# Moving the first chunk's gate into the second chunk, and reordering the loads of w_mod, q and the third chunk, in a long-convolution and token-mixer kernel

## The chip, the cores and the metric

The kernel runs on one core of a Trainium2 chip. The core has a matrix engine (TensorE, PE in the profile, with its weight loads as PEld), a vector engine (VectorE, DVE), a scalar engine (ScalarE, ACT), a general engine (GpSimd, POOL) and a queue engine that issues transfers (SyncE, SP). Each works through its own list of instructions in order; they wait for one another by semaphores. The metric is the device time of one execution in microseconds. Before the change the median of three runs was 666.49 us (665.19 to 666.98). One further execution was taken with the hardware profiler: 671.21 us, of which 669.4 us are the span that the trace covers.

## The reference

Everything is float32, one batch, 2048 tokens, 640 channels. What is computed, cut to what matters:

```python
mod = (silu(c) @ w_mod).reshape(1, 6, 1, 640)            # six rows: sa, ca, ga, sb, cb, gb
h = layernorm(q) * (1 + ca) + sa
k_shift = sum(k shifted by t, times shift_k[:, t])        # four taps along the tokens
kv = k_shift * v
y = irfft(rfft(kv, 4096) * rfft(ssm_k, 4096))[:2048] + kv * ssm_D
x = q + ga * (h * y)
h = layernorm(x) * (1 + cb) + sb
x = x + gb * token_mlp(h)                                 # 2048 -> 1728 -> 2048 along the tokens, gelu between
```

The change touches only the first half, up to `x = q + ga * (h * y)`.

## The kernel before, in words

The 640 channels are five **chunks** of 128. The long convolution of a chunk is a transform of length 64 by 32, done with small matrix products on TensorE. A chunk goes through these stages; all of them are small Python functions that append instructions to the engines' lists, so the order in which they are called is the order on each engine (no scheduler changes it).

- `kv_ops` (VectorE, and one group in four on GpSimd) multiplies the taps, sums, and multiplies by v: eight instructions for each of four groups; the result lies in the tile `x` (X in the code).
- `step1(0, t)`, t = 0 to 3 (line 230): first forward step on kv. `step1(1, t)`: the same on the filter, which `perm` (line 177, ScalarE) has permuted from the tile `aux` (KSR) into `p` after `perm_add` (GpSimd) has put ssm_D into its first element. ScalarE evacuates each step to `z` (line 235).
- `f2(g)`, g = 0 to 7 (line 249): the second forward step, called the products below. For each group ScalarE copies one half to `kt` (line 255), VectorE makes two products into `p` (two buffers of it in turn), GpSimd adds them to `y`. So VectorE's product of group g waits for GpSimd's addition of group g - 2. Between the products VectorE works off a list `fill`, a share of it in each group: in the first, second and third chunk this is `kv_ops` for the next chunk.
- `i2(0)`, `i2(1)` (line 280): the inverse by 32 in two halves, evacuated by ScalarE (line 288). `i1(0)`, `i1(1)` (line 300): the inverse by 64.
- `gate`: VectorE multiplies that result by a tile A1, which holds layernorm(q) for the chunk, scaled and shifted by two rows G1 and G0; then q gets it added, and `spill` writes the chunk's columns out.

A1 comes from 16 ScalarE copies (line 307) with the statistics of q as scale and bias, and two passes of VectorE over it with G1 and G0. G0 and G1 come from w_mod: `mod_part` (line 364) multiplies five row blocks of w_mod by silu(c), `mod_sum` (line 368) copies the sum out, `mod_row` (lines 375 to 384) spreads a row over the partitions. The statistics of q (bn_stats, line 600) are 48 VectorE instructions, and `rstd` turns them into scale and bias (a square root on ScalarE, then five small VectorE instructions).

TensorE's results lie in three PSUM tiles used in rotation (`psum()`), so a stage waits until the tile three stages back is read. A1 is one half of the tile `aux`, the filter (KSR) the other; w_mod's third and fourth blocks were loaded over both.

SyncE issues nearly all loads, strictly in order. In the first chunk it issues q (32 transfers), w_mod (five), the second inverse matrix `v1`, the second chunk's filter, then k and v of the third chunk. All forward and inverse stages of chunk c and the forward steps of chunk c + 1 are called in the loop body of chunk c.

Of the kernel before, what the change touches and what calls it, by code (L numbers as in the profile page):

```python
# [11 lines left out]
AF = mybir.ActivationFunctionType  # L12
ALU = mybir.AluOpType

S, D, F = 2048, 640, 1728
DC = 128
# [34 lines left out]
def mixer_kernel(ctx: ExitStack, tc: tile.TileContext, q, k, v, shift_k, ssm_k, ssm_D, w1, b1, w2, b2, c,  # L51
# [462 lines left out]
    all_taps()  # L514
    load_taps(2)
# [10 lines left out]
    three = lambda t: [t[:, 640 * j:640 * j + 640] for j in range(3)]  # L526
    pl = [three(t) for t in (T_v1, T_v1[:, 1920:3840], T_aux, T_aux[:, 2048:3968], P)]

    def load_q():
        for j in range(16):  # L530
            for b in range(2):
                sync.dma_start(XH[j // 8][64 * b:64 * b + 64, j % 8], dram(q, (16 * b + j) * D, [[32 * D, 64], [1, D]]))  # L532
        for kk in range(4):
            mod_load(0, kk, (T_v1[:, 0:1920], T_v1[:, 1920:3840], T_aux[:, 0:1920], T_aux[:, 2048:3968])[kk])
# [8 lines left out]
    for c in range(NC):  # L543
# [3 lines left out]
        for g in range(8):  # L547
# [21 lines left out]
            if c == 0 and g < 4:  # L569
                lay_w2(1, g)  # L570
                if g == 3:
                    load_q()
# [24 lines left out]
        if c == 0:  # L597
            for j in range(16):
                for h in range(2):
                    dve.bn_stats(bst[:, j, h, :], XR(j, 320 * h, 320))  # L600
                dve.bn_aggr(mv[:, j, :], bst[:, j, 0:2, :])
# [4 lines left out]
        if c == 0:  # L606
            mod_load(0, 4, P[:, 0:1920])
            for t in range(4):
                step1(0, t)
            ps = psum()  # L610
            pe.transpose(ps[:, 0:36], stg, ID[0:36, 0:36])
            act.activation(cols, ps[:, 0:36], AF.Copy)
            act.activation(sil, cols[:, 30:35], AF.Silu)
            i2(0)
            for kk in range(4):
                mod_part(tap, kk, pl[kk])
                if kk == 1:
                    sync.dma_start(T_v1[:, 0:4096], c_v1, max_dma_last_dim=4096)
                if kk == 2:
                    load_ks(1)  # L620
            rstd(rs1, nm1, 0, 16)
            run(ac[0:4])
            i2(1)
            mod_part(tap, 4, pl[4])
# [9 lines left out]
            mod_sum(tap, T_kt[:, 0:640])  # L634
            run(ac[4:8])
# [3 lines left out]
            for i in range(3):  # L639
                mod_row(i, T_kt[:, 0:640])  # L640
            run(ac[8:16])
            run(po)
            perm(1)
            taps()
            load_taps(3)
            load_ks(2)
            fill.extend(kv(3, ((0,), (1, 2), (3,))))
        elif cn is not None:
            for t in range(2):
                step1(0, t)  # L650
# [58 lines left out]
        if c == 0:  # L709
            add_x(c, 0)  # L710
            add_x(c, 1)
        spill(c)
        if c:
            k0()
        for t in range(1 if c else 0, 4):
            step1(1, t)
        if cn == NC - 1:
            dv(12)
            fill.extend(x1s(c, j) for j in range(16))
        else:  # L720
            dv(11 if c else 8)
# [505 lines left out]
```

## Time and profile before

| what | value |
|---|---|
| median of three runs | 666.49 us (665.19 to 666.98) |
| profiled execution | 671.21 us, span 669.4 us |
| TensorE matmul busy in the span | 619.5 us (93%) |
| VectorE busy | 501.9 us (75%) |
| ScalarE busy | 309.7 us (46%) |
| GpSimd busy | 108.1 us (16%) |
| mean granted TensorE clock | 0.982 of full |

These shares are means over the whole program. In the page's strip of 40 slices TensorE is below nine tenths only within the first thirteen; the five chunks run there, and the token MLP after them keeps it busy to the end. A row of the timeline gives the start in us, the length in us, the engine, the line, the operation, the tiles written and read, the shapes and how many instructions were merged; in brackets the idle time before it and what ended it. A row of the chain of waits gives start, length and what the chain ran through.

### The profile page before, as it was taken

Reading aid. Unit: us, or ns where it says so; the run is one execution under the profiler, and the core shown is the slowest. Engines: PE = TensorE matmul, PEld = TensorE weight load, DVE = VectorE, ACT = ScalarE, POOL = GpSimd, SP = SyncE. Lnnn points to the kernel's source line nnn. Section 1 sums busy time; section 2 is a strip of 40 time slices with the busy share of each in tenths; the row PEclk is TensorE's granted clock in tenths of the full one; section 3 lists DMA queues with packets and bytes.
Section 4 is the critical chain, followed back from the end, with each engine's and each line's share of the span. In section 5 each row is a group of like instructions: output and inputs, shape, how many; then the busy total and the mean of one; then the engine's idle time right before and its main releaser. Section 6 shows DMA issues by size and latency. Waiting matters only on the chain.

```text
span 669.4 us, 20749 instructions
## 1 busy us (share of the span) xinstructions
PE 619.5 (93%) x9073; PEld 597.8 (89%) x9073; DVE 501.9 (75%) x860; ACT 309.7 (46%) x483; POOL 108.1 (16%) x120
## 2 busy tenths in 40 slices
PE   0599878899998999999999999999999999999997
PEld 0598568788997989689999999999999999999997
DVE  6688569969969948789974213846689889888886
ACT  0574475545735647667765224334243332333331
POOL 5284027413324127000000000000000000000000
PEclk9999789999999999879999999999999999999999
DMA  9968988727438525414006630885598565345601
GB/s 179 213 194 225 391 172 159 168 54 165 83 70 221 180 51 156 172 33 95 0 1 126 119 71 1 189 234 144 174 365 268 173 179 154 102 144 169 188 31 41
DMA packets 175472, 98.01 MB, mean 146 GB/s; under 512 B 89843, under 2 KB 165398, under 8 KB 175126
## 3 DMA queue, kind: packets, MB, share of 16 engines
q1 hardware_dynamic: 170834, 95.38, 54.0%
q10 hardware_dynamic: 4548, 1.31, 1.1%
q8 instruction: 71, 1.16, 0.7%
q14 instruction: 19, 0.16, 0.1%
HBM read 79.63 MB, written 19.14 MB: 148 GB/s over the span
## 4 chain that ended last, share of the span: by engine, by line
PE 71%; DVE 16%; DMA 6%; issue 3%; SPq 2%; ACT 1%; POOL 0%; ACTq 0%; DVEq 0%; POOLq 0%
PE pst L1128 26%; PE pst L463 19%; PE pst L230 9%; PE pst L249 7%; PE pst L280 5%; PE pst L993 4%; DVE tap L60 3%; DVE kt L60 2%; DMA aux<-in_A_ssm_k_dram 2%; PE pst L300 2%; DMA aux<-in_w_mod_dram 2%; DVE p L60 1%; SPq L532 1%; PE tap L364 1%; DMA in<-in_A_k_dram 1%
## 5 line engine op out<-in xcount | busy, mean ns | idle before, releaser
L249 PE MATMUL pst<-z,w 128*64 128x64 f32 x2560 | 78.9, 223 | 11.0 <-DVE p L60 6.0
L249 PEld LDWEIGHTS pst<-z,w 128*64 128x64 f32 x2560 | 76.8, 138 | 13.7 <-issue 10.4
L230 PE MATMUL pst<-v,x 128*64 128x128 f32 x640 | 45.7, 302 | 24.2 <-DVE x L60 23.7
L230 PEld LDWEIGHTS pst<-v,x 128*64 128x64 f32 x640 | 43.6, 221 | 24.9 <-POOL t L488 23.7
L235 ACT ACTIVATE z<-pst 128x1024 f32<-128x1024 f32 (+2 forms) x45 | 41.4, 931 | 43.6 <-PE pst L230 24.9
L60 POOL TENSOR_TENSOR y<-p 128x256 f32<-128x256 f32 x72 | 54.1, 776 | 40.1 <-DVE p L60 39.7
L60 DVE TENSOR_TENSOR p<-pst,kt 128x512 f32<-128x512 f32 x80 | 50.8, 681 | 10.5 <-ACT kt L255 9.6
L280 PEld LDWEIGHTS pst<-v,y 32*128 32x128 f32 x1280 | 39.4, 193 | 4.2 <-issue 2.7
L280 PE MATMUL pst<-v,y 32*128 32x64 f32 x1280 | 41.2, 279 | 1.6 <-issue 1.0
L255 ACT ACTIVATE kt<-pst 128x512 f32<-128x512 f32 x40 | 23.9, 598 | 36.7 <-PE pst L249 20.9
L230 PE MATMUL pst<-v,p 128*64 128x128 f32 x640 | 37.3, 274 | 1.4 <-ACT p L177 1.2
L230 PEld LDWEIGHTS pst<-v,p 128*64 128x64 f32 x640 | 35.3, 137 | 2.2 <-ACT p L177 1.4
L1128 PE MATMUL pst<-r_z,m_w 128*128 128x320 f32 x198 | 37.2, 309 | 0.0
L60 DVE TENSOR_TENSOR tap<-tap,kt 128x512 f32<-128x512 f32 x51 | 35.5, 696 | 1.3
L60 DVE TENSOR_TENSOR kt<-in,tap 128x512 f32<-128x512 f32 x51 | 34.9, 685 | 1.5
L300 PEld LDWEIGHTS pst<-z,v 64*64 64x64 f32 x1280 | 24.7, 157 | 7.9 <-issue 3.5
L1128 PEld LDWEIGHTS pst<-r_z,m_w 128*128 128x128 f32 x198 | 31.1, 188 | 0.0
L300 PE MATMUL pst<-z,v 64*64 64x64 f32 x1280 | 26.9, 243 | 3.7 <-issue 2.4
L288 ACT ACTIVATE z<-pst 128x512 f32<-128x512 f32 x38 | 21.3, 664 | 18.3 <-PE pst L280 18.3
L1065 ACT ACTIVATE m_w<-m_v 128x896 fp32r<-128x896 f32 x19 | 17.9, 948 | 23.3 <-DVE m_v L60 13.0
L60 DVE TENSOR_TENSOR m_w<-m_v,m_w 128x896 fp32r<-128x896 f32 x19 | 20.6, 1086 | 6.5 <-ACT m_w L1065 6.5
L1128 PE MATMUL pst<-h_x,m_w 128*128 128x320 f32 x132 | 24.6, 309 | 0.0
(303 smaller groups left out, 1417.2 us busy)
## 6 DMA issues: line engine op xcount, KB each, us to landing
x<-in_B_w_dram SPq DMA_DIRECT2D x18, 512.0 KB
m_v<-in_B_w_dram SPq DMA_DIRECT2D x20, 384.0 KB
aux<-in_A_ssm_k_dram SPq DMA_DIRECT2D x10, 512.0 KB
out_dram<-m_w SPq DMA_DIRECT2D x32, 160.0 KB
in<-in_A_k_dram SPq DMA_DIRECT2D x36, 128.0 KB
in<-in_A_v_dram SPq DMA_DIRECT2D x36, 128.0 KB
ts<-m_p SPq DMA_DIRECT2D x10, 320.0 KB
m_w<-xs SPq DMA_DIRECT2D x20, 160.0 KB
```

The costliest lines, as they stand in the source:

```text
L60: TT = lambda eng, o, a, b, op: eng.tensor_tensor(o, a, b, op=op)
L230: pe.matmul(ps.rearrange("p (b m a) -> p b a m", b=2, a=4)[64 * ri:64 * ri + 64, a // 4, a % 4], lhs, F1[:, 128 * ri:128 * ri + 128], star ...
L235: act.activation(Z[:, side, t, :, k0:k1], ps.rearrange("p (b k a) -> p b k a", b=4, a=4)[:, :, k0:k1], AF.Copy)
L249: pe.matmul(pk[64 * h:64 * h + 64, kk // 4, ri, kk % 4], W2[k1 // 32][:, 2 * (k1 % 32) + ri], rhs, start=True, stop=True)
L255: act.activation(halves_(kt), pv[:, :, 1], AF.Copy)
L280: pe.matmul(pp[qd // 2][:, o:o + 64], Y[p, ri, i:i + 2].rearrange("p i k -> p (i k)"), V2[p, 64 * ri:64 * ri + 64], start=ri == 0, stop=ri ...
L288: act.activation(o, i, AF.Copy)
L300: pe.matmul(ps[64 * b:64 * b + 64, 512 * e + 64 * jj:512 * e + 64 * jj + 64], V1[p, ri, n2], T2[p, :, 32 * ri + n2], start=ri == 0, stop=r ...
L463: pe.matmul(ps[0:m, h, 0:320], w_.bitcast(F32R), r_[:, 320 * h:320 * h + 320].bitcast(F32R), start=first and i == 0, stop=last and i == 2)
L993: pe.matmul(ps[n][:, h, 0:320], sets[n][:, j].bitcast(F32R), r[:, 320 * h:320 * h + 320].bitcast(F32R), start=j == 0 and r is hh, stop=j = ...
L1065: act.activation(W[n][0].bitcast(F32R), A[p, w_], AF.Copy)
L1128: pe.matmul(bank[n], w[:, i].bitcast(F32R), r.bitcast(F32R), start=m == 0 and k == 0, stop=m == 6 and k == 2)
```

## The change

- The five w_mod blocks are loaded before q, into the place of `v1`, into half of q's own place (`xa`) and into A1's place; the second chunk's filter is loaded right after them. q comes after the third chunk's k and v, its second half of rows first (QJ), and after it k and v of the fourth chunk and the third chunk's filter.
- The sum over w_mod now stands in one piece in front of the first chunk's inverse, in a PSUM tile of the rotation.
- The first chunk's inverse by 64 is not gated. ScalarE copies it to A1's place (line 734). The statistics of q are taken in the second chunk: nine rows of tokens ahead of its products, seven as `fill`. `kv_ops` for the third chunk moves from `fill` to the time before the second chunk's products.
- After the second chunk's products, `rstd` runs, and ScalarE makes 16 copies for the first chunk (`late_rows`, line 549) into the free tiles `t` and `kt`; VectorE gates with them (`late_gate`, six instructions), GpSimd adds to q, `spill(0)` follows. Then come the second chunk's own 16 copies into A1, which before stood two by two between its products.

```diff
     all_taps()
+    PL = (T_v1[:, 0:1920], T_v1[:, 1920:3840], T_x[0][:, 0:1920], T_x[0][:, 1920:3840], T_aux[:, 2048:3968])
+    pl = [three(t) for t in PL]
+    for kk in range(5):
+        mod_load(0, kk, PL[kk])
+    load_ks(1)
     load_taps(2)
...
+    QJ = (*range(8, 16), *range(8))
     def load_q():
-        for j in range(16):
+        for j in QJ:
...
+    def late_rows(half):
+        for i in range(8):
+            j = 8 * half + i
+            act.activation(G_[half][:, i], XR(j, 0, DC), AF.Identity, scale=rs1[:, j:j + 1], bias=nm1[:, j:j + 1])
+    def late_gate(half):
+        a = G_[half]
+        g = lambda G: G[:, None, 0:DC].to_broadcast([128, 8, DC])
+        TT(dve, a, a, g(G1), ALU.mult)
+        TT(dve, a, a, g(G0), ALU.add)
+        av = a.rearrange("p j (m e) -> p e j m", e=2)
+        y = T_aux[:, 2048 + 1024 * half:3072 + 1024 * half]
+        TT(dve, av, y.rearrange("p (e j m) -> p e j m", e=2, j=8), av, ALU.mult)
+        x = XH[half][:, :, 0:DC]
+        TT(pool, x, x, a, ALU.add)
...
-            if c:
+            if c > 1:
                 n_ = 2 if cn is not None else 3
                 for f_ in ac[n_ * g:n_ * g + n_]:
                     f_()
...
             taps()
             load_taps(3)
+            ps = psum()
+            pe.transpose(ps[:, 0:36], stg, ID[0:36, 0:36])
+            act.activation(cols, ps[:, 0:36], AF.Copy)
+            act.activation(sil, cols[:, 30:35], AF.Silu)
+            for t in range(4):
+                step1(0, t)
+            ps = psum()
+            for kk in range(5):
+                mod_part(ps, kk, pl[kk])
+                if kk == 1:
+                    sync.dma_start(T_v1[:, 0:4096], c_v1, max_dma_last_dim=4096)
+            load_q()
+            mod_sum(ps, T_kt[:, 0:640])
+            perm(1)
+            i2(0)
+            for i in range(2):
+                mod_row(i, T_kt[:, 0:640])
+            ops = kv(3, ((0,), (1, 2), (3,)))
+            run(ops[0:16])
+            mod_row(2, T_kt[:, 0:640])
+            i2(1)
+            run(ops[16:])
             load_ks(2)
-            fill.extend(kv(3, ((0,), (1, 2), (3,))))
+            for j in QJ[0:9]:
+                run(q_stats(j))
+            for j in QJ[9:]:
+                fill.extend(q_stats(j))
         elif cn is not None:
-            for t in range(2):
-                step1(0, t)
+            if c == 1:
+                rstd(rs1, nm1, 0, 16)
+            step1(0, 0)
+            if c == 1:
+                late_rows(0)
+            step1(0, 1)
+            if c == 1:
+                late_rows(1)
+                for half in range(2):
+                    late_gate(half)
+                spill(0)
+                run(ac)
             perm(cn)
...
             ps = i1(half)
+            if c == 0:
+                act.activation(T_aux[:, 2048 + 1024 * half:3072 + 1024 * half], ps, AF.Copy)
+                continue
```

**Where the instructions stand now.** On SyncE, after the small loads of the first chunk (line 511 loads c), the queue before went on like this; lines 532 and 537 load q, 357 w_mod, 618 and 650 the matrix v1, 165 and 167 ssm_D and the filter, 161 the taps, 145, 151 and 156 k and v:

```order
L511 DMA g<-in_c_dram 5x128
L161 DMA rows<-in_A_shift_k_dram 64x256 x2
L532 DMA xa<-in_A_q_dram 64x640 x16
L532 DMA xb<-in_A_q_dram 64x640 x16
L357 DMA v<-in_w_mod_dram 128x3x640 x2
L357 DMA aux<-in_w_mod_dram 128x3x640 x2
L357 DMA p<-in_w_mod_dram 128x3x640
L618 DMA v<-in_const_v_dram 128x4x1024
L165 DMA rows<-in_A_ssm_D_dram 1x64 x2
L167 DMA aux<-in_A_ssm_k_dram 64x64x32 x2
```

The same place in the changed kernel:

```order
L511 DMA g<-in_c_dram 5x128
L357 DMA v<-in_w_mod_dram 128x3x640 x2
L357 DMA xa<-in_w_mod_dram 128x3x640 x2
L357 DMA aux<-in_w_mod_dram 128x3x640
L165 DMA rows<-in_A_ssm_D_dram 1x64 x2
L167 DMA aux<-in_A_ssm_k_dram 64x64x32 x2
L161 DMA rows<-in_A_shift_k_dram 64x256 x2
L145 DMA in<-in_A_k_dram 64x8x64 x4
L151 DMA in<-in_A_v_dram 64x8x64 x2
```

w_mod and the second chunk's filter have moved past all of q, and the taps of the third chunk (161) now stand behind the filter.

Further on in the same queue of the changed kernel, from the second half of q to the third chunk's filter:

```order
L537 DMA xa<-in_A_q_dram 64x640 x16
L151 DMA in<-in_A_v_dram 64x8x64 x2
L156 DMA in<-in_A_k_dram 63x3x64 x2
L145 DMA in<-in_A_k_dram 64x8x64 x2
L151 DMA in<-in_A_v_dram 64x8x64 x2
L145 DMA in<-in_A_k_dram 64x8x64 x2
L151 DMA in<-in_A_v_dram 64x8x64 x2
L145 DMA in<-in_A_k_dram 64x8x64 x2
L151 DMA in<-in_A_v_dram 64x8x64 x2
L145 DMA in<-in_A_k_dram 64x8x64 x2
L165 DMA rows<-in_A_ssm_D_dram 1x64 x2
L167 DMA aux<-in_A_ssm_k_dram 64x64x32 x2
```

Ahead of this filter load (167) now stand 32 transfers of q and 18 of the fourth chunk's k and v; before, it followed directly on the taps of line 161 and had the 18 behind it.

On ScalarE, from the last copy of the second chunk's products (line 255) to the evacuation of its second inverse half, before:

```order
L255 ACTIVATE kt<-pst_1618 128x512
L307 ACTIVATE aux<-xb,sm 128x128 x2
L183 ACTIVATE tap<-rows 128x256
L235 ACTIVATE z<-pst_1669 128x1024
L235 ACTIVATE z<-pst_1687 128x1024
L177 ACTIVATE p<-aux 128x32x2x32
L288 ACTIVATE z<-pst_1713 128x4x2x64 x2
L288 ACTIVATE z<-pst_1714 128x4x2x64 x2
L235 ACTIVATE z<-pst_1785 128x1024
```

and with the change:

```order
L183 ACTIVATE tap<-rows 128x256
L348 ACT_TABLE_LOAD
L348 ACTIVATE sm<-sm 128x16
L235 ACTIVATE z<-pst_1628 128x1024
L549 ACTIVATE t<-xa,sm 128x128 x8
L235 ACTIVATE z<-pst_1654 128x1024
L549 ACTIVATE kt<-xb,sm 128x128 x8
L307 ACTIVATE aux<-xa,sm 128x128 x8
L307 ACTIVATE aux<-xb,sm 128x128 x8
L177 ACTIVATE p<-aux 128x32x2x32
L288 ACTIVATE z<-pst_1716 128x4x2x64 x2
L288 ACTIVATE z<-pst_1717 128x4x2x64 x2
```

The square root, the 16 late copies (549) and the second chunk's 16 copies (307) now all stand in front of the evacuation of the first inverse half (288); before, none of them did.

More of the change, by code (lines that the diff above doesn't have):

```diff
@@ L514, in mixer_kernel @@
     all_taps()
+    three = lambda t: [t[:, 640 * j:640 * j + 640] for j in range(3)]
+    PL = (T_v1[:, 0:1920], T_v1[:, 1920:3840], T_x[0][:, 0:1920], T_x[0][:, 1920:3840], T_aux[:, 2048:3968])
[3 more added lines that the diff above has]
+    load_ks(1)
     load_taps(2)
@@ L596, in mixer_kernel @@
             pa_next()
[L597 to L601, printed above, removed]
         if c and c + 2 < NC:
```

45 lines of the change are left out of this document (8 added, 37 removed).

## The prediction

> **What bounds the kernel now.** I read the chain of waits over the first 260 us, then each engine's timeline around the two places that the change touches: the passage from the first chunk to the second, and the end of the second. The chain in the first passage:
>
> ```profile
> 66.39 10.95 DMA aux<-in_w_mod_dram
> 77.39 1.31 PE tap L364 x12
> ...
> 79.40 11.78 DMA aux<-in_A_ssm_k_dram
> ...
> 94.48 0.78 POOL aux L60
> 95.28 2.19 ACT p L177
> ...
> 97.51 4.03 PE pst L230 x65
> ```
>
> TensorE waits for w_mod, which is queued behind q, and then for the second chunk's filter, queued behind w_mod. TensorE's own rows:
>
> ```profile
> 41.36 14.18 PE L249 MATMUL pst<-z,w 128*64 128x64 f32 x476 [0.37 <-ACT z L235]
> 57.71 8.29 PE L230 MATMUL pst<-v,x 128*64 128x128 f32 x128
> 77.39 1.28 PE L364 MATMUL tap<-aux,sm 128*32 128x320 f32 x12 [0.43 <-DMA aux<-in_w_mod_dram]
> 87.70 1.37 PE L375 MATMUL pst<-kt,sm 1*128 1x320 f32 x12 [1.61 <-ACT kt L368]
> 97.51 7.51 PE L230 MATMUL pst<-v,p 128*64 128x128 f32 x128 [1.24 <-ACT p L177]
> 105.39 1.79 PE L249 MATMUL pst<-z,w 128*64 128x64 f32 x54 [0.37 <-ACT z L235]
> ...
> 126.72 4.30 PE L230 MATMUL pst<-v,x 128*64 128x128 f32 x64 [0.44 <-DVE p L60]
> 130.95 3.80 PE L280 MATMUL pst<-v,y 32*128 32x64 f32 x128
> 136.91 4.04 PE L280 MATMUL pst<-v,y 32*128 32x64 f32 x128
> 143.13 2.10 PE L300 MATMUL pst<-z,v 64*64 64x64 f32 x128
> ...
> 156.30 0.92 PE L249 MATMUL pst<-z,w 128*64 128x64 f32 x24 [0.44 <-ACT z L235]
> ```
>
> Three lengths matter: 97.51 to the second chunk's products at 105.39; these products to the next kv step, 126.72 - 105.39 = 21.3 us (the first chunk took 57.71 - 41.36 = 16.4); from there to the first inverse by 64, 143.13 - 126.72 = 16.4.
>
> **Term 1, the first passage.** The changed queue differs first at 37.74:
>
> ```profile
> 37.74 4.03 SPq L161 DMA_DIRECT2D rows<-in_A_shift_k_dram  x2
> 41.81 11.35 SPq L532 DMA_DIRECT2D xa<-in_A_q_dram  x16
> 53.20 11.97 SPq L532 DMA_DIRECT2D xb<-in_A_q_dram  x16
> ...
> 97.83 2.66 SPq L151 DMA_DIRECT2D in<-in_A_v_dram  x4
> ...
> 105.85 4.13 SPq L167 DMA_DIRECT2D aux<-in_A_ssm_k_dram  x2
> GB/s 413 406 410 410 330 218 212 54 34 39 209 217 183 155 143 159 219 124 174 216 192 198 139 174 173 162 54 125 193 205 52 162 205 128 113 160 261 274 225 166
> ```
>
> The last row is one number per us from 80 to 120. It gives 400 GB/s for w_mod and v1 (until 84.4), 215 for a filter half (2.5 us for 512 KB), and a pause between the halves. The second transfer of the five w_mod blocks takes the slot on which the old queue stood until 41.8, so four blocks of 0.98 MB flow from 43 to 52.8; the filter's halves follow, to about 55.3 and 61; the third chunk's taps, issued behind it, land near 62. ScalarE's taps copy stands ahead of its evacuations, so ScalarE stands until then; taps, small copy, table load and silu take 2.3, one evacuation 1.0, and the fourth kv step starts at 65.3 and ends at 67.4 (66.0 before). ScalarE's rows for what follows:
>
> ```profile
> 84.92 2.17 ACT L288 ACTIVATE z<-pst 128x512 f32<-128x512 f32 x4 [2.63 <-PE pst L280]
> 86.93 0.72 ACT L368 ACTIVATE kt<-tap 96x640 f32<-96x640 f32 x1
> 89.08 0.70 ACT L382 ACTIVATE g<-pst 128x640 f32<-128x640 f32 x1
> 90.27 3.18 ACT L307 ACTIVATE aux<-xb,sm 128x128 f32<-128x128 f32 x8
> ...
> 129.03 1.03 ACT L235 ACTIVATE z<-pst 128x1024 f32<-128x1024 f32 x1 [0.40 <-PE pst L230]
> 131.97 2.08 ACT L177 ACTIVATE p<-aux 128x2048 f32<-128x2048 f32 x1
> ```
>
> From 67.4: five w_mod parts of 1.28, 6.4; inverse half 3.8; its evacuation 2.2; copies of G0 and G1 1.4, for which the second half now waits since it needs their PSUM tiles; second half 3.9; evacuation 2.2; two inverses by 64, 4.0. That is 91.3, and the filter is long there: perm, 2.1, lies under the inverse, mod_sum's 0.72 beside it. Against 97.51 term 1 is **-6.2**, products at 99.2. Below, if TensorE pays only for its own work (8.3, 6.4, 3.8, 1.4, 3.9, 2.2, 4.0 from 57.7), it is 87.7, -9.8; above, with the taps 4 us later, -2.
>
> **Term 2, the second chunk's products.** VectorE's rows:
>
> ```profile
> 44.12 1.29 DVE L60 TENSOR_TENSOR p<-pst,kt 128x512 f32<-128x512 f32 x2 [1.72 <-ACT kt L255]
> ...
> L600 DVE BATCH_NORM_STATS2 sm<-xa 128x6 f32<-128x320 f32 x16 | 6.8, 465 | 0.0
> L601 DVE BATCH_NORM_AGGREGATE sm<-sm 128x2 f32<-128x12 f32 x16 | 3.4, 210 | 0.5
> ```
>
> The first product comes 2.75 us after the start. Up to the sixth, whose PSUM tile the next kv step needs, there are six pairs of 1.29 and 17 of the 21 statistics instructions, 5.7 (a row of tokens is 3 instructions, 1.0 us). 2.75 + 7.7 + 5.7 = 16.2, against 21.3: **-5.1**. VectorE has the nine earlier rows done by 98: kv_ops, then the gate rows at 82, then 5.8 and 9. Bounds: -5 (the first chunk's 16.4) to -6 below, -3.5 above if q is late. The kv step would stand at 115.4.
>
> **Term 3, GpSimd and the third chunk's filter.** In the queue: taps, 18 transfers of k and v at 0.68 (2.66 for four with their gaps), 12.3, taps 1.2, v1: about 71.5. Then 23.4 for q at the two rows' pace, 2.4 while the eighth transfer stands behind v1's 2 MB, 12.3 for k and v, 0.7: the filter is issued at 110.3. By the bandwidth row the old one, issued at 105.85, had flowed by 113.3, 7.5 later; the new lands at 117.8. Who needs it:
>
> ```profile
> 111.25 1.42 POOL L60 TENSOR_TENSOR y<-p 128x256 f32<-128x256 f32 x2 [1.96 <-DVE p L60]
> ...
> 115.87 0.78 POOL L60 TENSOR_TENSOR aux<-aux,rows 1x64 f32<-1x64 f32 x2
> ```
>
> These two additions into the filter (perm_add) stand in GpSimd's list ahead of the third group's addition, and before they waited for nothing. The fifth product needs that addition's buffer: 117.8 + 0.4 + 0.7 = 118.9, where VectorE would have been ready at 115.4 - 3.6 = 111.8. Queued behind it are the statistics, the last products, and TensorE's next tile. **+7.1**. Bounds: 0, with the queue at 0.64 per transfer and no stand behind v1 (landing near 112), to +9. I take the row's pace.
>
> **Term 4, the end of the second chunk.** From the kv step, t: two more products 2.6, GpSimd's share of the last additions on VectorE 0.9, the five small rstd steps 1.5:
>
> ```profile
> 76.39 0.26 DVE L339 RECIPROCAL sm<-sm 128x16 f32<-128x16 f32 x1 [0.38 <-ACT sm L348]
> ...
> 77.69 0.18 DVE L353 SCALAR_TENSOR_TENSOR sm<-sm 128x16 f32<-128x16 f32 x1
> ...
> 91.41 4.92 DVE L60 TENSOR_TENSOR aux<-aux,g 128x1024 f32<-128x1024 f32 x4
> ...
> 98.51 1.97 DVE L60 TENSOR_TENSOR xa<-xa,aux 128x1024 f32<-128x1024 f32 x1
> ...
> 128.88 0.89 DVE L60 TENSOR_TENSOR y<-p 128x128 f32<-128x128 f32 x4
> ```
>
> Scale and bias stand at t + 5.0 (the square root lies under the products). Then ScalarE alone: eight late copies 3.3, an evacuation 1.0, eight more 3.3, to 12.6; the second chunk's first eight to 15.9; its last eight wait for the second late gate, three VectorE operations of 1.23 from 12.6, one of them beside a GpSimd addition and so nearer to 1.97 to 2.3 than to 1.23, 17.3; to 20.6, perm to 22.7, evacuation to 24.9. The second inverse half needs the tiles so freed; 6.2 us later (143.13 - 136.91) the inverse by 64 starts, t + 31.0 against 16.4: **+14.6**. None of it is covered: TensorE has one kv step in between, and the kv_ops and gates of VectorE stand behind the same copies. Before, the 16 copies lay between the products, where ScalarE had room. Bounds: +12.9 with copies of 0.40 and no wait for the gate, +16.
>
> [...]
>
> **The sum.** -6.2 - 5.1 + 7.1 + 14.6 = +10.4. From the inverse by 64 on, the order is the old one and so is each wait, so it passes to the end.
>
> ```profile
> span 669.4 us, 20749 instructions
> ```
>
> This execution took 671.21 us, 4.7 above the median of 666.49; the terms are differences and hold for both. I forecast 676.9, and 681.6 for an execution like the profiled one.
>
> **Rivals.** (a) The filter is in time: term 3 is 0, the sum +3.3, 669.8. For it: the old additions found the filter landed; against it: 50 transfers stand ahead. (b) The other side: TensorE pays in the first passage for its own work alone and the products run without a stand: 95.6 for their start, 16.2 for their length, 111.8 against 126.72, -14.9; with term 4 at its lower bound, +12.9, it is -2.0: 664.5. It decides if VectorE's and SyncE's waits fall under TensorE's work; against it, the evacuations between the inverses stand in the rows above. (c) The early loads cost: the taps of the third chunk, behind 4.9 MB and a filter, hold ScalarE 4 us longer: 681. (d) The change does nothing where it says: if w_mod and filter were still last, term 1 would be 0 and the sum +16.6; the new order makes that unlikely, and it falls under (c).
>
> **How the numbers follow.** Forecast 0.55, (a) 0.17, (b) 0.20, (c) with (d) 0.08. A measurement here tells from no change what is over 0.3%, 2 us. (a) lies near that bound: a third of it counts as no change; (b) lies on it, and half of it does. Faster 0.10, same 0.16, slower 0.74. The range reaches down into (b), to 665, and up past (c), to 683.
>
> **What would show it.** Right: no wait for w_mod, the filter step near 91; perm_add on GpSimd held until 117 by the filter's transfer; TensorE idle some 14 us before the second inverse half, ended by ScalarE's line 288; the third chunk's products near 167 instead of 156.3; unchanged lengths behind. Wrong: an inverse by 64 of the second chunk before 143, or ScalarE's 32 copies spread out.

## The result, and the profile after

| | median | runs | ratio to before, 95% interval |
|---|---|---|---|
| before | 666.74 us | 4 | |
| changed | 707.37 us (705.98 to 710.34) | 4 | 1.0593 (1.0558 to 1.0627) |

The four runs of before are the three above and one more. The change makes the kernel 40.6 us slower; 10.4 were forecast, and the range ended 24 us below the result. A few executions of some versions ran at a lower granted clock and over 1% longer; the ratios below leave these out, the medians do not. The profiled execution took 705.98 us, with a span of 704.2 and a mean granted clock of 0.959 (0.982 before). The prediction's marks, in us from the span's start:

| mark | before | predicted | after |
|---|---|---|---|
| second chunk's kv step ends | 66.0 | 67.4 | 89.1 |
| second chunk's products begin | 105.39 | 99.2 | 127.74 |
| products to the third chunk's kv step | 21.3 | 23.3 | 19.5 |
| kv step to the inverse by 64 | 16.4 | 31.0 | 35.3 |
| second chunk's inverse by 64 | 143.13 | 153.5 | 182.56 |
| third chunk's products begin | 156.30 | 166.7 | 194.56 |

At the inverse by 64 the loss is 39.4 us: 22.35 from the first passage, -1.8 from the products, 18.9 from the end of the second chunk. TensorE's timeline of the changed kernel, to be held against the one of before:

```profile
41.43 6.75 PE L249 MATMUL pst<-z,w 128*64 128x64 f32 x222 [0.37 <-ACT z L235]
49.51 3.95 PE L249 MATMUL pst<-z,w 128*64 128x64 f32 x127 [1.33 <-issue]
56.69 6.52 PE L249 MATMUL pst<-z,w 128*64 128x64 f32 x163 [3.23 <-issue]
...
78.62 10.49 PE L230 MATMUL pst<-v,x 128*64 128x128 f32 x128 [15.23 <-POOL x L60]
...
102.02 7.34 PE L280 MATMUL pst<-v,y 32*128 32x64 f32 x121
...
144.52 2.99 PE L249 MATMUL pst<-z,w 128*64 128x64 f32 x64 [2.64 <-DVE p L60]
147.24 4.83 PE L230 MATMUL pst<-v,x 128*64 128x128 f32 x64
...
170.91 0.69 PE L280 MATMUL pst<-v,y 32*128 32x64 f32 x4 [12.83 <-ACT z L288]
171.92 7.09 PE L280 MATMUL pst<-v,y 32*128 32x64 f32 x124 [0.31 <-ACT z L288]
178.94 3.69 PE L230 MATMUL pst<-v,x 128*64 128x128 f32 x32
182.56 2.25 PE L300 MATMUL pst<-z,v 64*64 64x64 f32 x128
```

Four things stand in it. The kv step (line 230) waits 15.23 us for a write of `x` by GpSimd; it waited for nothing before. The first chunk's products have two stands (stretches in which TensorE does nothing) for which the row names only "issue"; before there was one, of 1.07 us. The second inverse half (line 280) waits 12.83 us for ScalarE. And rows that carry no wait, or next to none, have grown: the kv step from 8.29 to 10.49 us, an inverse half from 3.8 or 4.0 to 7.34 and 7.09, a quarter of the kv step (178.94) from 2.28 to 3.69.

The first wait, on GpSimd's timeline of the changed kernel:

```profile
66.13 1.09 POOL L635 TENSOR_SCALAR t<-rows 128x256 f32<-128x256 f32 x1
...
68.03 2.48 POOL L60 TENSOR_TENSOR t<-in,t 128x512 f32<-128x512 f32 x2
...
77.30 1.26 POOL L60 TENSOR_TENSOR x<-t,in 128x512 f32<-128x512 f32 x1
...
138.13 0.35 POOL L60 TENSOR_TENSOR aux<-aux,rows 1x64 f32<-1x64 f32 x1 [2.77 <-DMA aux<-in_A_ssm_k_dram]
141.81 0.35 POOL L60 TENSOR_TENSOR aux<-aux,rows 1x64 f32<-1x64 f32 x1 [3.33 <-DMA aux<-in_A_ssm_k_dram]
```

The eight instructions from 68.03 on are GpSimd's group of the third chunk's `kv_ops`. In the changed program they are called ahead of `step1(0, t)`, so TensorE's kv step waits for their write of `x` at 77.30, although it belongs to the next chunk. TensorE stands from 63.4 on; until 66.2 GpSimd still adds products, until 68.0 it works on its own taps and the filter, and the group takes 10.5 us. GpSimd is busy for 14.1 of these 15.2 us: TensorE waits for its work, not for a transfer, and experiment four bears that out. There is only one buffer of `x`. So the group also overwrites a quarter of the second chunk's kv before the kv step has read it, and the changed kernel computes the second chunk there from the third chunk's kv. Experiments two, three, four and six keep this order; the others leave the second chunk its own kv. The last two rows are the additions of term 3, held by the third chunk's filter as forecast, for 6.1 us in all; TensorE's share of that is the 2.64 in its row at 144.52.

ScalarE at the end of the second chunk, and VectorE beside it:

```profile
151.66 3.19 ACT L549 ACTIVATE t<-xa,sm 128x128 f32<-128x128 f32 x8 [0.38 <-issue]
...
155.66 3.19 ACT L549 ACTIVATE kt<-xb,sm 128x128 f32<-128x128 f32 x8
158.74 3.18 ACT L307 ACTIVATE aux<-xa,sm 128x128 f32<-128x128 f32 x8
164.74 3.19 ACT L307 ACTIVATE aux<-xb,sm 128x128 f32<-128x128 f32 x8 [2.82 <-DVE kt L60]
167.84 2.02 ACT L177 ACTIVATE p<-aux 128x2048 f32<-128x2048 f32 x1
169.76 2.10 ACT L288 ACTIVATE z<-pst 128x512 f32<-128x512 f32 x4
```

```profile
154.88 2.48 DVE L60 TENSOR_TENSOR t<-t,g 128x1024 f32<-128x1024 f32 x2 [3.31 <-ACT t L549]
157.40 1.23 DVE L60 TENSOR_TENSOR t<-aux,t 128x1024 f32<-128x1024 f32 x1
158.88 4.57 DVE L60 TENSOR_TENSOR kt<-kt,g 128x1024 f32<-128x1024 f32 x2 [0.25 <-ACT kt L549]
```

This is term 4's queue in the forecast order: 16 late copies, eight copies, a wait for the late gate, eight copies, `perm`, and only then the evacuation on which TensorE stands. The late gate's row at 158.88 takes 4.57 us for two instructions, where the row at 154.88 takes 2.48. In the chain of waits the first of the two has 3.32 us, 2.1 more than the 1.23 of the others; GpSimd's late addition (158.76, 2.34 us) runs beside it.

The grown rows, in busy time by stretch of the changed kernel (after the span of a stretch: busy time of TensorE, its weight loads, VectorE, ScalarE, GpSimd; then the granted clock, DMA share, GB/s):

```profile
36.00:56.00 20.00, 15.75 (x442) 15.23 (x438) 15.72 (x25) 11.39 (x15) 15.84 (x17) 1.00 1.03 319
...
78.60:89.10 10.50, 10.48 (x131) 10.36 (x134) 0.00 (x0) 3.08 (x3) 0.00 (x0) 0.74 0.01 2
102.00:109.40 7.40, 7.37 (x126) 7.00 (x124) 6.41 (x10) 0.38 (x1) 0.00 (x0) 0.50 1.06 255
...
171.90:179.00 7.10, 7.08 (x126) 6.97 (x126) 2.29 (x1) 1.20 (x2) 0.00 (x0) 0.50 0.01 2
```

The kv step ran at 0.74 and both inverse halves at 0.50 of the clock; the clock stayed at 0.50 to 182.60, over the quarter of the kv step that follows. The kv step and the last half stand behind a long wait of TensorE. Ahead of the half at 102.02 TensorE was busy for 3.51 of 3.6 us (98.4 to 102.0), but with 19 matmuls only. Before, the kv step took 8.29 us, the inverse halves 3.8 to 4.0 and the quarter 2.28, at 1.00 of the clock. Together that is 2.2 + 3.4 + 3.2 + 1.4 = 10.2 us. In the first row TensorE is busy 15.75 of 20 us while transfers take all of the DMA engines: the stands in the products.

From the third chunk's products to the end the profiled executions differ by 3.5 us less than up to there (38.3 at the products, 34.8 in the span). The profiled one of before had a stretch at half the clock, which the other lacks; it goes the right way, and its size was not worked out:

```profile
280.00:290.00 10.00, 9.45 (x200) 6.54 (x198) 5.45 (x18) 5.20 (x10) 0.00 (x0) 0.50 0.01 2
```

That execution was also 4.47 us above its median, and the changed one 1.39 below; 34.77 + 4.47 + 1.39 is the 40.6 of the medians.

### The profile page after: what moved, and what is told of

Same layout as the page of the kernel before. It is cut to its first block, busy times and chain, and to the rows that moved or that the text cites. A ratio compares the mean times of both kernels' runs of the same rounds, so it can differ in the third digit from the quotient of the medians.

```text
span 704.2 us, 20762 instructions
## 1 busy us (share of the span) xinstructions
PE 626.1 (89%) x9073; PEld 607.5 (86%) x9073; DVE 500.7 (71%) x858; ACT 310.8 (44%) x485; POOL 110.4 (16%) x122
## 4 chain that ended last, share of the span: by engine, by line
PE 65%; DVE 16%; DMA 7%; ACT 4%; SPq 4%; issue 3%; POOL 2%; ACTq 0%; DVEq 0%; POOLq 0%
PE pst L1157 24%; PE pst L463 18%; PE pst L230 8%; PE pst L249 5%; PE pst L1022 3%; PE pst L280 3%; PE pst L300 2%; DVE kt L60 2%; DVE p L60 2%; DVE tap L60 2%; DMA xb<-in_A_q_dram 1%; POOL t L60 1%; SPq L151 1%; DMA aux<-in_A_ssm_k_dram 1%; DVE aux L60 1%
## 5 line engine op out<-in xcount | busy, mean ns | idle before, releaser
L249 PE MATMUL pst<-z,w 128*64 128x64 f32 x2560 | 81.2, 226 | 12.9 <-issue 6.6
L249 PEld LDWEIGHTS pst<-z,w 128*64 128x64 f32 x2560 | 79.0, 141 | 15.6 <-issue 12.3
L230 PE MATMUL pst<-v,x 128*64 128x128 f32 x640 | 49.7, 322 | 38.6 <-DVE x L60 23.4
L230 PEld LDWEIGHTS pst<-v,x 128*64 128x64 f32 x640 | 47.6, 221 | 39.2 <-POOL t L488 23.3
L60 DVE TENSOR_TENSOR p<-pst,kt 128x512 f32<-128x512 f32 x80 | 51.1, 682 | 29.5 <-ACT kt L255 26.2
L280 PEld LDWEIGHTS pst<-v,y 32*128 32x128 f32 x1280 | 45.2, 214 | 17.0 <-ACT z L288 13.5
L280 PE MATMUL pst<-v,y 32*128 32x64 f32 x1280 | 47.5, 301 | 14.0 <-ACT z L288 13.1
L60 DVE TENSOR_TENSOR x<-tap,in 128x512 f32<-128x512 f32 x17 | 11.7, 690 | 28.2 <-PE pst L230 27.8
L300 PEld LDWEIGHTS pst<-z,v 64*64 64x64 f32 x1280 | 22.2, 142 | 8.1 <-issue 3.0
L300 PE MATMUL pst<-z,v 64*64 64x64 f32 x1280 | 24.0, 228 | 5.1 <-ACT z L288 2.0
```

Source lines behind the costliest of these rows:

```text
L60: TT = lambda eng, o, a, b, op: eng.tensor_tensor(o, a, b, op=op)
L230: pe.matmul(ps.rearrange("p (b m a) -> p b a m", b=2, a=4)[64 * ri:64 * ri + 64, a // 4, a % 4], lhs, F1[:, 128 * ri:128 * ri + 128], star ...
L249: pe.matmul(pk[64 * h:64 * h + 64, kk // 4, ri, kk % 4], W2[k1 // 32][:, 2 * (k1 % 32) + ri], rhs, start=True, stop=True)
L280: pe.matmul(pp[qd // 2][:, o:o + 64], Y[p, ri, i:i + 2].rearrange("p i k -> p (i k)"), V2[p, 64 * ri:64 * ri + 64], start=ri == 0, stop=ri ...
L300: pe.matmul(ps[64 * b:64 * b + 64, 512 * e + 64 * jj:512 * e + 64 * jj + 64], V1[p, ri, n2], T2[p, :, 32 * ri + n2], start=ri == 0, stop=r ...
```

## The experiments

Ratios are to the kernel before on the same chip. By their intervals, a difference between two of them is uncertain by 5 to 6 us. The theories: **A**, GpSimd's third-chunk group holds the kv step. **B**, the third chunk's filter holds GpSimd in the products (term 3). **C**, the granted clock falls after a stretch in which TensorE does little, and TensorE pays behind it. **D**, ScalarE's late copies hold the end of the second chunk (term 4). **E**, w_mod's transfers slow the first chunk's products.

**One: GpSimd's group behind the kv step.**

```diff
-            run(kv_ops(2, pool))
             taps()
...
             for t in range(4):
                 step1(0, t)
+            run(kv_ops(2, pool))
```

> Edit: the changed kernel with GpSimd's eight instructions for the third chunk's kv group called after the second chunk's four kv steps, not before. (In the changed kernel they overwrite one of the four groups of the second chunk's kv before its steps read it, so the changed kernel computes that group of the second chunk from the third chunk's data; here it doesn't.) Theory A (the kv step waits for GpSimd's group, which waits for the third chunk's k and v): the step starts when the products end, near 63, not at 78.6; 15 us less there, all later marks some 15 to 18 earlier, total 690 +- 4. Theory B (the step waits for the loads as such, or for the taps copy on ScalarE, which ends at 66): the step starts at 63 to 66 only if the taps are in; total 695 to 703 if something else takes the wait's place.

Measured: 694.21 us, 1.0349 (1.0271 to 1.0427). TensorE's timeline of this run:

```profile
62.57 8.31 PE L230 MATMUL pst<-v,x 128*64 128x128 f32 x128 [0.17 <-DVE p L60]
...
83.53 7.08 PE L280 MATMUL pst<-v,y 32*128 32x64 f32 x124
...
108.22 12.14 PE L249 MATMUL pst<-z,w 128*64 128x64 f32 x394 [0.43 <-ACT z L235]
...
129.13 3.68 PE L249 MATMUL pst<-z,w 128*64 128x64 f32 x64 [6.50 <-DVE p L60]
```

The kv step's wait is 0.17 instead of 15.23 and its length 8.31 again; the products start 19.5 us earlier. A is shown; by the ratios it cost 16 us (0.0244 of 667). The inverse half at 83.53 still takes 7.08 us. Some 3.9 us of the wait come back as the longer wait for the filter, 6.50 against 2.64, close to the 7.1 forecast for it.

**Two: the clock, first try.** Idle matmuls of 64x128 on TensorE in three of its waits.

```diff
+    def spin(n):
+        for _ in range(n):
+            pe.matmul(tap[0:64, 768:896], V2[:, 0:64], F1[:, 0:128], start=True, stop=True)
```

> Edit: the changed kernel with idle matmuls on TensorE (64x128, into a part of a PSUM tile that nothing reads) in three of its waits: 200 ahead of the second chunk's kv steps, 30 ahead of the rows of w_mod, 190 ahead of the second chunk's second inverse half. Theory C (after an idle stretch the granted clock is down to 0.5 to 0.8, and the next stage runs slow): kv steps 10.5 -> 8.3 us, the first chunk's second inverse half 7.3 -> about 4, the second's 7.1 -> about 4, total 707.4 - 7 = 700 +- 3. Rival (the long rows come from waits inside, or the clock falls whatever TensorE does): rows as long as before or total 707 or more, by as much as the idle matmuls overrun the waits.

Measured: 774.45 us, 1.1524 (1.1417 to 1.1630). The matmuls took 0.22 us each and overran the waits: 200 of them took 43.8 us from 62.98 on, and the last 190 began at 196.77, since VectorE was reading their PSUM tile. So the time says nothing on C. The rows behind the idle matmuls do:

```profile
106.69 8.08 PE L230 MATMUL pst<-v,x 128*64 128x128 f32 x127
...
133.49 4.78 PE L280 MATMUL pst<-v,y 32*128 32x64 f32 x124 [0.16 <-ACT g L384]
...
240.40 3.80 PE L280 MATMUL pst<-v,y 32*128 32x64 f32 x128
```

8.08 instead of 10.49, 4.78 instead of 7.34, 3.80 instead of 7.09. The first ran at 1.00 of the clock (106.7 to 114.8), the second at 0.77 (133.4 to 138.3). The last has the length of the inverse half at 130.95 in the trace of before, which ran at 1.00 (126.7 to 143.1).

**Three: without late copies, late gate and late additions.** This version leaves out the gate of the first chunk.

```diff
-            if c == 1:
-                late_rows(0)
             step1(0, 1)
             if c == 1:
-                late_rows(1)
-                for half in range(2):
-                    late_gate(half)
                 spill(0)
                 run(ac)
```

> Edit: the changed kernel without the 16 late copies on ScalarE, the six late gate operations on VectorE and the two additions on GpSimd: the first chunk's gated result is left out of the output. Theory D (ScalarE's list ahead of the evacuation of the inverse sets the end of the second chunk): from the third chunk's kv step to the inverse by 64 the 35.3 us become about 35.3 - 6.4 - 3.5 (wait for the late gate) - 1 = 24 to 26, total 707.4 - 10 = 697 +- 3. Rival (VectorE's own work there or the wait for statistics sets it): less than 4 us are won.

Measured: 697.80 us, 1.0423 (1.0360 to 1.0486).

```profile
145.20 4.30 PE L230 MATMUL pst<-v,x 128*64 128x128 f32 x64
...
159.72 0.69 PE L280 MATMUL pst<-v,y 32*128 32x64 f32 x4 [4.25 <-ACT z L288]
160.73 7.09 PE L280 MATMUL pst<-v,y 32*128 32x64 f32 x124 [0.32 <-ACT z L288]
...
171.37 2.32 PE L300 MATMUL pst<-z,v 64*64 64x64 f32 x128
```

In TensorE's timeline 26.2 us instead of 35.3 from the kv step to the inverse by 64, and the wait for ScalarE 4.25 instead of 12.83. By the ratios D cost 11 us. D is shown for these; the second chunk's own 16 copies, still ahead of the evacuation, are left with the 4.25 and a half still at 7.09.

**Four: w_mod behind the third chunk's k and v.**

```diff
-    for kk in range(5):
-        mod_load(0, kk, PL[kk])
     load_ks(1)
...
             load_v(2, 3)
+            for kk in range(5):
+                mod_load(0, kk, PL[kk])
```

> Edit: the changed kernel with the five w_mod loads behind the third chunk's k and v, still ahead of q. Theory E (while w_mod's 4.9 MB keep the transfer engines full, TensorE's first products stand twice, 1.3 and 3.2 us, for something that the profile doesn't name): the two stands shrink to 1 us or less, the products end near 58.5 instead of 63.2; GpSimd's group starts some 10 us earlier as its k and v land earlier, so the kv step starts near 65 to 68 instead of 78.6; total 707.4 - 10 to - 14 = 695 +- 4. Rival (the stands belong to the place in TensorE's list and not to the transfers): they stay, the products still end at 63, and only GpSimd's group comes earlier.

Measured: 702.15 us, 1.0494 (1.0417 to 1.0570).

```profile
40.40 15.15 PE L249 MATMUL pst<-z,w 128*64 128x64 f32 x512 [0.38 <-ACT z L235]
...
70.97 9.65 PE L230 MATMUL pst<-v,x 128*64 128x128 f32 x128 [15.24 <-POOL x L60]
```

All 512 matmuls of the products stand in one row of 15.15 us, where the changed kernel has three with 1.33 and 3.23 us between them. E is shown as far as that the stands go with these transfers; by the ratios it cost 7 us. What holds TensorE then is open. From 40 to 64 us in the changed kernel the DMA engines moved, beside the loads, five packets of the kind instruction (queue and kind, packets, MB, share). Before, these were five too, with one stand of 1.07 us, and in this run four, with none; no run tested whether the stands have to do with them:

```profile
q1 hardware_dynamic: 12672, 6.10, 94.8%
q8 instruction: 5, 0.08, 1.5%
```

The time forecast for this run, 695, was missed: the wait for GpSimd is as long as in the changed kernel. k and v now come ahead of w_mod, but GpSimd's group still starts only when GpSimd is done with its work ahead of it, as it did at 68.03 in the changed kernel:

```profile
60.38 2.49 POOL L60 TENSOR_TENSOR t<-in,t 128x512 f32<-128x512 f32 x2
```

**Five: the filter between the halves of q**, on top of the first.

```diff
-            load_q()
+            load_q(QJ[0:8])
             mod_sum(ps, T_kt[:, 0:640])
             perm(1)
+            load_ks(2)
+            load_q(QJ[8:])
```

> As the run with GpSimd's third-chunk group behind the kv step (median 694.2 us, 1.035 of the kernel before), and besides that the third chunk's filter is loaded between the two halves of q instead of behind all of q and 18 transfers of k and v. Theory B (the prediction's term 3: the additions into that filter hold GpSimd, and through it VectorE and TensorE, inside the second chunk's products): the row TensorE 129.13 us with 6.50 us idle ahead of it goes, the second chunk's products take 17 to 18.5 us up to the kv step instead of 24.3, and the ratio falls by 0.009 to about 1.026. Rival: the second half of q then lands some 4 us later and its statistics hold VectorE in the same products; the wait only changes its name and the ratio stays within 0.003 of 1.035.

Measured: 685.53 us, 1.0247 (1.0199 to 1.0296).

```profile
108.39 8.03 PE L249 MATMUL pst<-z,w 128*64 128x64 f32 x267 [0.43 <-ACT z L235]
...
124.18 4.39 PE L230 MATMUL pst<-v,x 128*64 128x128 f32 x64
```

The stand of 6.50 is gone from TensorE's timeline, and the products take 15.8 us (124.18 - 108.39) instead of 24.3. B is shown, at 6.8 us by the ratios. q's later second half held nothing.

**Six: the clock, second try**, with so few idle matmuls that they end inside the waits, written into the tile of the step that follows.

```diff
-    def step1(side, t, later=False):
+    def step1(side, t, later=False, n=0):
         ps = psum()
+        spin(ps, n)
...
-                step1(0, t)
+                step1(0, t, n=64 if t == 0 else 0)
...
-            step1(0, 2)
+            step1(0, 2, n=52 if c == 1 else 0)
```

> The changed kernel with idle matmuls on TensorE in its two long waits: 64 of them (0.22 us each, 14.0 us) in the 15.2 us ahead of the second chunk's kv step, and 52 (11.4 us) in the 12.8 us ahead of the second inverse half of that chunk, each into a PSUM tile that the next stage writes over. Nothing else is changed, so no wait becomes shorter. Theory C (the granted clock falls to half after such a wait, and TensorE pays for it behind the wait): kv step 8.3 us instead of 10.49, second inverse half of the second chunk 3.9 instead of 7.09, the first chunk's second inverse half, in whose short wait nothing is put, still 7.3; 5.4 us less in all, ratio 1.051 against 1.059. Rival (the low clock comes from something else, power or time, and idle matmuls do not change it): the same lengths, ratio 1.059 or more.

Measured: 709.83 us (705.41 to 715.36), 1.0632 (1.0575 to 1.0689). TensorE's timeline (lines have moved by five):

```profile
78.22 8.37 PE L235 MATMUL pst<-v,x 128*64 128x128 f32 x128 [0.96 <-POOL x L60]
...
100.33 7.08 PE L285 MATMUL pst<-v,y 32*128 32x64 f32 x124
...
169.66 4.91 PE L285 MATMUL pst<-v,y 32*128 32x64 f32 x124 [0.57 <-ACT z L293]
174.49 3.71 PE L235 MATMUL pst<-v,x 128*64 128x128 f32 x32
```

The two stages behind the filled waits took 8.37 and 4.91 us (10.49 and 7.09 in the changed kernel); the half of the first chunk, where nothing was put in, took 7.08. So the rows bear C out, with a limit: the quarter of the kv step at 174.49 is as long as without the idle matmuls (3.71 and 3.69, the latter at 0.50 of the clock). What exactly lowers the clock is open. The sum does not bear C out: the fifth chunk's products began 4.1 us earlier in the profiled execution (284.54 against 288.65), yet it took 705.41 us in all, 0.6 less, and the timed runs, which spread over 10 us, show no gain. What the lower clock costs in the end is not shown by a time.

**Seven: the three waits taken away together**, the filter of the fifth and the third's omission on top of the first. The first chunk's gate is left out here too.

> The changed kernel with the three waits taken away one on the other: GpSimd's third-chunk group behind the kv step, the third chunk's filter between the halves of q, and the late copies, the late gate and its additions left out, so that the first chunk's gate is missing from the output. The second chunk's 16 copies still stand ahead of the inverse's evacuation, w_mod is still loaded early, and the half clock in the first chunk's inverse is still there. If the three add up: 26 us (35.3) from the kv step to the inverse by 64 as in the run without the late gate alone, so 9 to 11 us less than the version with two of them (ratio 1.0247): ratio 1.009 to 1.011. Rival: with the filter early, something hidden so far takes their place (the 16 copies themselves, or the fourth chunk's k and v, which stand behind q); ratio 1.015 or more.

Measured: 675.14 us, 1.0146 (1.0093 to 1.0200). From the kv step (123.96) to the inverse by 64 (149.61) it took 25.7 us, so the waits add up in the profile; the time's interval holds both what they and what the rival gave. Left over are the 16 copies with a wait of 4.22, the stands in the first products, and two inverse halves at 7.12 and 7.09.

**Eight to ten: all of it reordered.** Each diff shows only a part of its version. The first reworked version loads w_mod behind the third chunk's k and v, puts the inverse by 32 ahead of the w_mod products that come last, and spreads the late copies.

```diff
-    PL = (T_v1[:, 0:1920], T_v1[:, 1920:3840], T_x[0][:, 0:1920], T_x[0][:, 1920:3840], T_aux[:, 2048:3968])
+    PL = (T_v1[:, 0:1920], T_v1[:, 1920:3840], T_x[1][:, 0:1920], T_x[1][:, 1920:3840], T_aux[:, 2048:3968])
...
+            if c == 1:
+                if g == 2:
+                    rstd(rs1, nm1, 0, 16)
+                if g > 2:
+                    late_rows(0, (range(0, 3), range(3, 6), range(6, 8), (), ())[g - 3])
+                if g in (5, 6, 7):
+                    lg.pop(0)()
```

> A version in which all that was found is taken away together: w_mod is loaded behind the third chunk's k and v and into places that leave q's first half free, q's first half follows at once and the filter stands behind q's second half but ahead of k and v of the fourth chunk; GpSimd's third-chunk group stands behind the kv step; the inverse by 32 stands ahead of the w_mod products that come last; the scale and bias of q are formed within the second chunk's products (third group), with the first half of the late copies and of the late gate; the second half of the late copies and the second chunk's copies stand between the evacuations at the end of the chunk instead of ahead of them. If the three waits (kv step, filter, ScalarE's 32 copies) and the half clock behind them are the whole loss: products of the second chunk from about 95 (127.7 in the changed kernel), 20 us for them because VectorE has more in them, 18 us from the kv step to the inverse by 64 (35.3), that is about 133 there (182.6), ratio 0.985. If something else carries the loss (q itself too late, VectorE full): the inverse by 64 at 145 or later and the ratio at 1.005 or more.

Measured: 695.18 us, 1.0381 (1.0323 to 1.0439). The ratio forecast was 0.985. One new wait was the longest: the one for the matrix v1, queued behind q's first half, whose issue alone took 19.56 us (11.35 in the kernel before).

```profile
96.01 3.50 PE L300 MATMUL pst<-z,v 64*64 64x64 f32 x141 [11.89 <-DMA v<-in_const_v_dram]
```

The second version issues v1 ahead of q, and mends the order on VectorE and GpSimd.

```diff
             sync.dma_start(T_v1[:, 0:4096], c_v1, max_dma_last_dim=4096)
+            load_q(range(8))
             i2(1)
```

> The reworked version again, with what its first run showed mended: the matrix v1 (which came at 96 us and held TensorE for 11.9 us) is issued ahead of q instead of behind its first half; VectorE does all of the third chunk's kv work ahead of the rows of w_mod; GpSimd's late additions stand behind those of the products; the second half of the second chunk's gate rows stands behind the first half's gate. If those were what kept it slow: the first chunk's inverse by 64 at about 82 us (96), products of the second chunk at 97 to 99 (113.1), their kv step at 116 to 118 (131.3), the inverse by 64 of the second chunk at 135 to 137 (159.1; 143.1 in the kernel before), ratio 0.99. Rival: with q behind v1 the statistics run into the products and ScalarE's 24 copies behind the products still stand in TensorE's way with the half clock behind each wait; inverse by 64 at 145 or later, ratio 1.005 or more.

Measured: 668.36 us (10 runs), 1.0001 (0.9970 to 1.0031).

```profile
99.99 4.30 PE L249 MATMUL pst<-z,w 128*64 128x64 f32 x140 [0.43 <-ACT z L235]
...
117.96 4.33 PE L230 MATMUL pst<-v,x 128*64 128x128 f32 x64
...
136.29 2.10 PE L300 MATMUL pst<-z,v 64*64 64x64 f32 x128 [1.38 <-ACT z L288]
...
149.16 5.82 PE L249 MATMUL pst<-z,w 128*64 128x64 f32 x192 [0.44 <-ACT z L235]
```

The same data are loaded, in another order, and the late gate is still in it. The marks of the second chunk are within a microsecond of the expected ones, but the ratio of 0.99 was missed. The loss of the change is gone, so it was one of order and not of the work moved. The third chunk's products begin 7.1 us ahead of the kernel before, but take 20.2 us against 16.5. The third version gives GpSimd a quarter of the fourth chunk's kv work.

```diff
                 step1(0, 3)
+                run(kv_ops(2, pool))
                 run(ac[12:16])
```

> The second reworked version (ratio 1.000, products of the third chunk at 149.16 us against 156.30 in the kernel before, but 20.2 us long against 16.5, since VectorE came into them with ten instructions of the fourth chunk's kv work still to do), and besides that one of the four groups of that kv work on GpSimd, which does little there. If VectorE's backlog is what gave the lead back: products of the third chunk 17 us or less, those of the fourth chunk at 193 to 195 (201.58 before, 197.78 in the second reworked version), 3 us less, ratio 0.995. Rival: GpSimd's eight instructions beside VectorE's lengthen these (a gate row took 2.48 us alone and 4.53 for two beside a GpSimd addition), and the ratio stays within 0.003 of 1.000.

Measured: 667.02 us (12 runs), 0.9998 (0.9973 to 1.0024). The third chunk's products took 16.9 us (151.96 to 168.87) but began 2.8 us later; the fourth's began at 197.68, 3.9 us earlier than in the kernel before, but no earlier than in the second version (197.78), where 193 to 195 had been forecast. No more than a tie comes of it, so the lead in the profiled execution is not in the times; where it goes is open. The kernel before's profiled execution, with its slow stretch, is a poor measure for the part behind.

## Why the prediction was wrong, and where it was right

The direction was right, the size was not. By the prediction's own steps:

**Term 1, the first passage: the step that failed.** It forecast -6.2 and was +22.35, 28.5 off. The step is the sentence that let the fourth kv step end at 67.4, with only the taps copy on ScalarE ahead of it. The kv step reads `x`, which GpSimd's group writes, and the new program calls that group first: the list of what a moved instruction waits for was not read through on GpSimd. This wait was put at nothing and was 15.23 us. The kv step ended at 89.1, 21.7 later: 5.7 because the first products ended late (3.5 by the stands, 4.56 against 1.07, and 1.8 by longer matmuls, 17.22 us against 15.45, with the clock at 0.79 from 56 to 64), 13.8 from GpSimd (15.2 less the 1.4 counted for the taps), 2.2 from the clock. Experiments four and one show the first two. The 1.4 for the taps was counted for nothing: in experiment one ScalarE copied them at 62.80 without a wait, and the kv step took 8.31 us. From there to the products 38.6 us passed instead of 31.8: 3.4 from the inverse half at 7.34, 2.8 from two stands of 1.13 and 1.68 in the inverse by 64 and the filter step, and 1.8 from the inverses by 64 themselves, less about 1 where steps ran shorter than counted. For these inverses the sum took 4.0 us, from the second chunk. The first chunk's own rows in the trace of before, at the same place in the order, had 5.83:

```profile
89.84 3.87 PE L300 MATMUL pst<-z,v 64*64 64x64 f32 x142 [0.76 <-ACT g L382]
94.32 1.96 PE L300 MATMUL pst<-z,v 64*64 64x64 f32 x114 [0.61 <-issue]
```

Rival (c) priced early loads that cost, but at 4 us and by the taps; (b), TensorE paying for its own work alone, was the furthest off.

**Terms 2 and 3, the products: right, and tested apart.** Without the filter's stand they take 15.8 us (experiment five), 16.2 forecast. The filter's stand, 7.1 forecast, was 6.50 where the first passage is cured of GpSimd's wait (experiment one). In the changed kernel it was 2.64, since the products began 28.5 us late, the filter's issue, at 132.6 instead of 110.3, 22.3, and the filter landed 9.1 us behind its issue where 7.5 were counted. Rival (a), the filter in time, falls.

**Term 4, the end of the second chunk: the queue on ScalarE right, what stands behind it 4.3 short.** 35.3 us instead of 31.0. The evacuation that ends the queue ended 24.6 us behind the start of the kv step, 24.9 forecast. That it fits so well is in part luck: the late gate beside GpSimd's addition lost 2.1 us where 1.0 was counted, but the late copies ended at 11.6 where 12.6 was counted. From the evacuation to the inverse by 64 passed 10.7 us instead of 6.2: 3.1 more for the second inverse half and 1.4 more for the quarter of the kv step, both at 0.50 of the clock, which no term contained. Experiment three took 9.1 us out of this stretch by taking the late part out.

**Behind the inverse by 64** the loss was handed on as forecast: 39.4 there, 38.3 at the third chunk's products.

That the clock is lower behind such a place could have been read in the profile of before, in the first chunk's inverses by 64, behind stands of 1.61 and 0.76 us and twelve short matmuls:

```profile
89.00:93.00 4.00, 3.24 (x131) 3.16 (x132) 3.11 (x4) 4.00 (x11) 0.35 (x1) 0.65 0.97 162
```

The range had no case in which GpSimd holds the kv step. By the ratios A costs 16 us, B 7, D 7 to 11, E 7, each uncertain by 5 to 6; nothing measures the clock's share, 10.2 us in the rows, by a time of its own, and part of it lies within these.

## What to carry to other kernels

When an instruction group is moved ahead of another, list for each tile that the later group reads who writes it now, on every engine, the idle ones too: here a buffer shared by two chunks turned GpSimd's work for the next chunk into a 15 us wait. Such a wait can also be a sign that the reader gets the wrong data, since the newer write now comes first. Look in the trace for stages that run at a lower clock behind stands, and leave room in a forecast for longer rows behind a new stand: here the kv step took 10.49 instead of 8.29 us behind one of 15.23 us, at 0.74 of the clock, and an inverse half 7.09 instead of 4.04 us behind one of 12.83 us, at 0.50. And try a copy on an engine that also evacuates PSUM behind or between the evacuations, not ahead of them: the late part cost 7 to 11 us ahead of them, and in the second reworked version, which has it within the products and between the evacuations, the kernel was level with the one before.

## What the runs showed of the hardware

- The granted clock was 0.50 over 10.7 us of nearly unbroken matmuls behind a stand of 12.8 us (171.90 to 182.60, busy 10.68 of 10.70). It was 0.50 over 7.4 us (102.0 to 109.4) behind 3.6 us without a stand but with only 19 matmuls. Straight behind idle matmuls of 0.22 us each that filled the stand, the inverse half took 3.80 us, the length of one at 1.00 in the trace of before (experiment two). Where waits of 1.58 and 0.57 us lay between, it took 4.91 us, and the quarter of the kv step behind it 3.71 us, against 3.69 at 0.50 in the changed kernel (experiment six).
- While w_mod came in, with the DMA engines' share at 1.03 (36 to 56 us), TensorE stood 1.33 and 3.23 us in the middle of a stage, for nothing that the profile names. It did not when those transfers ran later (experiment four). From 40 to 64 us loads took 94.8% of the DMA engines' time in the changed kernel and 73.6% in experiment four. What held TensorE is not shown.
- One VectorE instruction of 128x1024 with both inputs in SBUF took 3.32 us beside a GpSimd addition of 2.34 us; three others of this shape took 1.23 or 1.24 us with GpSimd idle (154.88 to 158.63). In the trace of before two of this shape took 1.97 and 2.30 us (98.51 and 100.40) beside GpSimd's group, of which two instructions took 2.14 us each there, and 1.28 or 1.29 us each from 103.91 on. VectorE's instructions of 128x512 took 0.68 to 0.70 us beside that group (102.62 to 108) and 0.69 to 0.70 us with GpSimd idle (129.69 to 134.7).
